# Weight conversion in a fused RWKV-6 and tanh-shrink kernel: the sign part is made by GpSimd instead of ScalarE

## The chip, the core and the metric

The kernel runs on one core of one Trainium2 chip. The metric is the device time of one launch in microseconds (us); lower is better. The engines are called by their profile names: PE is TensorE (PEld its weight loads), DVE is VectorE, ACT is ScalarE, POOL is GpSimd, and SP is SyncE, which here only starts DMAs.

## What is computed

Two blocks in sequence. The first is a linear-attention recurrence, the second a feed-forward block whose activation is `h - tanh(h)`.

```python
# r, k, v, w: (4, 8, 768, 48) float32;  u: (8, 48)
for t in range(S):
    cur = einsum('bhd,bhe->bhde', u[None] * kt, vt)
    y[:, :, t] = einsum('bhd,bhde->bhe', rt, state + cur)
    state = wt[:, :, :, None] * state + einsum('bhd,bhe->bhde', kt, vt)
x = y.transpose(0, 2, 1, 3).reshape(3072, 384)
h = x @ w_in                     # w_in (384, 2048)
out = (h - tanh(h)) @ w_out      # w_out (2048, 384)
```

The kernel is handed `w_in` and `w_out` as 64-bit words and makes float32 weights of them on the chip; that conversion is what the change is about.

## The kernel before

**Blocks and steps.** The 3,072 tokens are cut into eight blocks of 384. For each block, 16 feed-forward steps `f` run: `first` multiplies one slice of 128 columns of `w_in` with the block's `xT` (three matmuls of 384 columns, L871) and ScalarE copies the result out of PSUM as `h` (L876). VectorE squares it (`s`, L902), ScalarE makes `qa` of it (L905), VectorE makes `h` times a polynomial and then `g` from it (two instructions of L879), and TensorE multiplies `g` by a slice of `w_out` (L950 in the first block, a scheme with fewer products at L999 in the later ones). In the first block the second product of a step is queued three steps after its `g`. The attention work of the next block is laid between the steps: decay scans on VectorE (L417, L429), products (L436, L443, L382, L386), masked copies out of PSUM (L502), state updates (L587).

**Order.** PE, SP, DVE and ACT run in the order in which the program issues their instructions; it is written out by hand. Only POOL's queue is left to a scheduler; before the change it holds small fills, the drawing of masks, and three small DMAs (L777).

**The weights.** They arrive as 16 units of 768 columns (two slices of `w_in` or of `w_out`), one DMA each into a buffer `raw` (L251, five buffers), and stay in `w_sb` afterwards. All of this happens in the start-up (`boot`) and in the steps of the first block. A word of a unit has a low and a high half, each read with a stride of two 32-bit words. `convert` returns three ScalarE operations (L264) and one VectorE operation (L268) for a unit:

- `a`, into `w_sb`: the high half times `HIGH_SCALE`;
- `high`, a float16 in the one half of each word of a scratch tile `up` (four buffers): the high half times `SIGN_SCALE`, which leaves the sign;
- `low`, a uint16 in the other half of `up`: the low half scaled;
- on VectorE, `a` shifted left by three bits and joined with `up`, back into `w_sb`.

`converting(pieces, n)` issues the next `n` ScalarE operations of the units and says which VectorE operations have become due; those are issued in the next step, as `extra`. `PIECES` says how many operations each step of the first block issues. In `boot`, units 0 and 1 and most of unit 2 are converted.

Of the kernel before, what the change touches and what calls it, by code (L numbers as in the profile page):

```python
# [72 lines left out]
RAWS = 5  # L73
LAG = 2
LAST = 5
PIECES = 0, 0, 2, 3, 3, 3, 3, 4, 3, 3, 3, 4, 4
UNITS = [(0, 0), (0, 1)] + [u for j in range(NF // 2 - 2) for u in ((1, j), (0, j + 2))] + [(1, NF // 2 - 2),
                                                                                      (1, NF // 2 - 1)]
LATE = 3
# [47 lines left out]
def kernel(  # L127
# [12 lines left out]
    nc = tc.nc  # L140
# [112 lines left out]
    def convert(part, j, raw, _, tiles=1):  # L253

        lo, hi = raw[:, :, 0], raw[:, :, 1]
        a = w_sb[:, part, 2 * j:2 * j + 2].rearrange("p f c -> p (f c)").bitcast(I32)
        up = conv.tile([P, 2 * DM], I32, name="up", tag="up", bufs=4)
        low, high = (up.bitcast(t).rearrange("p (n two) -> p n two", two=2)[:, :, i]  # L260
                     for i, t in enumerate((U16, F16)))

        def scaled(to, of, scale, bias=0.0):
            return lambda: nc.scalar.activation(out=to, in_=of, func=AF.Copy, scale=scale, bias=bias)  # L264

        return [scaled(a.bitcast(F32), hi.bitcast(F32), HIGH_SCALE), scaled(high, hi.bitcast(F32), SIGN_SCALE),
                scaled(low, lo.bitcast(U32), *LOW)], [
                lambda of=slice(i * 2 * DM // tiles, (i + 1) * 2 * DM // tiles): nc.vector.scalar_tensor_tensor(  # L268
                    out=a[:, of], in0=a[:, of], scalar=3, in1=up[:, of], op0=ALU.logical_shift_left,
                    op1=ALU.bitwise_or) for i in range(tiles)]  # L270
# [49 lines left out]
    class Block:  # L320
# [411 lines left out]
        def together(self, ps):  # L732

            self.results(ps)
            yp, spread, St, ended = self.yp, isinstance(ps, Kept), states[self.q], {}

            def scores(p, c, h, par):
                toks = slice(64 * par, 64 * par + 64)
                return self.v[toks, c, p * D2 + h * D:p * D2 + (h + 1) * D], A[toks, h, p, c, :]

            def from_state(p, c, h, par):
                rows = slice(64 * h, 64 * h + D)
                return St[rows, p, 2 * c + par, 0:D], self.chunk("pre", p, 2 * c + par, spread)[rows]

            def stretch(of, cross):
                first = cross not in ended
                begun = set()
                for n in range(UP):
                    for c in range(NCP):
                        for h in range(2):  # L750
                            for x in range(2):
                                p, par = UP * n + x, x ^ cross
                                if of is from_state and not (self.q or c or par):
                                    continue
                                lhs, rhs = of(p, c, h, par)
                                e0, n0 = 64 * (h ^ x), (n * NCP + c) * L
                                done = nc.tensor.matmul(yp[x][e0:e0 + D, par, n0:n0 + L], lhsT=lhs, rhs=rhs,  # L757
                                                        start=first and (x, e0) not in begun, stop=True,
                                                        skip_group_check=True)
                                begun.add((x, e0))  # L760
                                if not first and len(begun) == 1:
                                    begin_behind(ended[cross], done)
                if first:
                    ended[cross] = nc.gpsimd.memset(ended_at, 0.0)
                    begin_behind(done, ended[cross])

            for of in (from_state, scores) if self.q else (scores, from_state):
                for cross in range(2):
                    stretch(of, cross)
            self.result_out(ALL)  # L770
            self.fill_holes([nc.sync])

        def fill_holes(self, engines, which=range(2 * KC)):
# [342 lines left out]
    def converting(pieces, n):  # L1116

        made = []
        for _ in range(n):
            if not pieces:  # L1120
                on_act, on_dve = convert(*raws.pop(0))
                pieces += zip(on_act, ([], [], on_dve))
            op, then = pieces.pop(0)
            op()
            made += then
        return made

    def boot(ps, pair, blk, later):
        h1, h2 = HALVES
        blk.tiles["w"] = states0  # L1130
        for name, p0, n in (("w", h1 + 1, 1), ("w", h1, 1), ("k", h1, UP), ("r", h1, UP), ("w", h2, UP)):
            blk.load(name, p0, n)
        blk.load_v()
        blk.load("k", h2, UP)
        blk.load("r", h2, UP)
        more_weights(nc.sync)

        both = (h1, h1 + 1), (h2, h2 + 1)
        blk.behind(h1 + 1, 1)
        blk.behind(h1, 1)  # L1140
        blk.take_whole(h1, UP)
        blk.totals_by_column(h1)
        nc.scalar.copy(out=later_ident, in_=ident)
        blk.before(h1, UP)
        blk.times_behind(h1, UP)
        blk.times_u(h1, UP)
        own = blk.own(ps, h1, spare=94, ahead=5, late=6)
        blk.turn_1(ps, h1)
        blk.times_before(h1, UP)
        earlier = blk.earlier(ps, h1)  # L1150
        blk.behind(h2, UP)
        blk.take_whole(h2, UP)
        first_a, first_b = convert(*raws.pop(0), tiles=2)
        own()
        blk.turn_2(h1)
        blk.totals_by_column(h2)
        blk.update_half(pair, h1)
        begin_behind(blk.done, more_weights(nc.sync))
        blk.times_behind(h2, UP)
        blk.times_u(h2, UP)  # L1160
        blk.turn_1(ps, h2)
        blk.turn_2(h2)
        earlier()
        blk.results(ps)
        blk.result("from_scores", both[0])
        run(blk.states_half(h1))
        blk.result("from_states", both[0], True, apart=True)
        blk.before(h2, UP)
        blk.update_half(pair, h2)
        blk.times_before(h2, UP)  # L1170
        own = blk.own(ps, h2)
        own_scored = blk.done
        run(first_a[:1])
        blk.result_out((3,), [nc.scalar.copy] * 2)
        blk.result_out((2,))
        earlier = blk.earlier(ps, h2, ahead=1)
        scored = blk.done
        onwards = blk.states_half(h2)
        own()
        run(first_a[1:])  # L1180
        needed = 2 * KC - 2
        blk.fill_holes([nc.sync, nc.gpsimd], range(needed, 2 * KC))
        begin_behind(own_scored, more_weights(nc.sync))
        blk.fill_holes([nc.sync, nc.gpsimd], range(needed))
        begin_behind(scored, more_weights(nc.sync))
        later.load("w")
        second_a, second_b = convert(*raws.pop(0))
        third_a, third_b = convert(*raws.pop(0))
        run(second_a)
        more_weights(nc.sync)  # L1190
        blk.results(ps)
        blk.yp.reverse()
        blk.result("from_states", both[1], apart=True)
        earlier(1, 1)
        earlier(0, 1)
        for p in reversed(both[1]):
            blk.result("from_scores", (p,), True, more=True)
        later.load("k")
        more_weights(nc.sync)
        run(onwards)  # L1200
        run(first_b[:1])
        for p in reversed(both[1]):
            blk.result_out((p,), [nc.scalar.copy, nc.vector.tensor_copy])
        run(first_b[1:])
        run(third_a[:2])
        run(second_b)
        blk.held(0, NPAIR)
        return [(third_a[2], third_b)]

    mains = ExitStack()  # L1210
    ps_a = Kept(mains.enter_context(tc.tile_pool(name="ps_a", bufs=1, space=PSUM)))
# [35 lines left out]
    for i, blk in enumerate(blocks):  # L1247
# [9 lines left out]
        for f in range(NF):  # L1257
# [21 lines left out]
            if not now:  # L1279
                ops = square + converting(pieces, 2)  # L1280
            elif now == 1:
                ops = rest + late + square + converting(pieces, 3)
            elif not i:
                ops = extra + square + (rest + behind + spare if f < 7 else rest[:1] + behind + spare + rest[1:])
            elif forming:
                ops = between(rest, forming[:2]) + square + formed + forming[2:]
                ops = (between(ops, behind) if len(behind) > 2 else ops + behind) + spare
            elif square:
                ops = (between(rest, behind) if len(behind) > 2 else rest + behind) + square + formed + extra + spare
            else:  # L1290
                ops = between(rest + formed, behind + spare)
# [161 lines left out]
```

## The times and the profile before

| what | value |
|---|---|
| median of 3 runs | 544.39 us (544.1 to 545.06) |
| the profiled execution, its own time | 545.07 us |
| its span in the trace | 543.3 us |
| granted TensorE clock | 1.0 throughout |
| PE busy | 534.1 us (98%) |
| DVE busy | 459.0 us (84%) |
| ACT busy | 403.7 us (74%) |
| POOL busy | 6.5 us (1%), 47 instructions |

The busy shares are means over stages that differ: the weights are converted in the first 80 us, and nothing of the change lies behind that. Matmuls are pipelined and their ends are modelled, so a busy PE says only that it had something in flight.

### The profile page before, as it was taken

Reading aid. Unit: us, or ns where it says so; the run is one execution under the profiler, and the core shown is the slowest. Engines: PE = TensorE matmul, PEld = TensorE weight load, DVE = VectorE, ACT = ScalarE, POOL = GpSimd, SP = SyncE. Lnnn points to the kernel's source line nnn. Section 1 sums busy time; section 2 is a strip of 40 time slices with the busy share of each in tenths; the row PEclk is TensorE's granted clock in tenths of the full one; section 3 lists DMA queues with packets and bytes.
Section 4 is the critical chain, followed back from the end, with each engine's and each line's share of the span. In section 5 each row is a group of like instructions: output and inputs, shape, how many; then the busy total and the mean of one; then the engine's idle time right before and its main releaser. Section 6 shows DMA issues by size and latency. Waiting matters only on the chain.

```text
span 543.3 us, 14866 instructions
## 1 busy us (share of the span) xinstructions
PE 534.1 (98%) x5682; PEld 403.3 (74%) x5682; DVE 459.0 (84%) x943; ACT 403.7 (74%) x814; POOL 6.5 (1%) x47
## 2 busy tenths in 40 slices
PE   7999999999999999999999999999999999999996
PEld 5756665678877777777887787877788788777874
DVE  7999999999989989798997979879797997557463
ACT  4899986888668876688767886688866885766561
POOL 1100000000000000000000000000000000000000
PEclk9999999999999999999999999999999999999999
DMA  7798732252311631154112532136321420100101
GB/s 276 234 402 311 259 119 74 97 137 63 122 42 54 162 118 57 43 147 119 60 56 87 122 103 70 48 97 151 84 89 46 122 27 3 56 1 0 45 1 46
DMA packets 53048, 56.34 MB, mean 104 GB/s; under 512 B 21488, under 2 KB 50928, under 8 KB 52976
## 3 DMA queue, kind: packets, MB, share of 16 engines
q1 hardware_dynamic: 52592, 55.18, 33.9%
q8 instruction: 48, 0.79, 0.6%
q14 instruction: 24, 0.20, 0.1%
q10 hardware_dynamic: 288, 0.10, 0.1%
q0 software_dynamic: 96, 0.07, 0.1%
HBM read 44.73 MB, written 4.72 MB: 91 GB/s over the span
## 4 chain that ended last, share of the span: by engine, by line
PE 88%; DVE 6%; ACT 2%; issue 2%; DMA 1%; SPq 0%; DVEq 0%
PE hp L871 41%; PE acc L999 27%; PE att L999 7%; PE att L757 4%; PE acc L950 3%; PE acc L977 2%; PE att L494 2%; PE att L575 1%; PE att L871 1%; ACT up L264 1%; DMA r<-in_rT 1%; DVE w_sb L268 1%; PE acc L871 1%; DVE scores L502 1%; DVE states L587 1%
## 5 line engine op out<-in xcount | busy, mean ns | idle before, releaser
L871 PE MATMUL hp<-xT,w_sb 128*128 128x384 f32 x738 | 259.3, 488 | 0.4 <-ACT h L876 0.4
L871 PEld LDWEIGHTS hp<-xT,w_sb 128*128 128x128 f32 x738 | 131.8, 190 | 70.0 <-ACT h L876 1.3
L999 PE MATMUL acc<-forms,g 128*128 128x128 f32 x954 | 133.2, 276 | 0.0
L876 ACT ACTIVATE h<-hp 128x384 f32<-128x384 f32 x123 | 60.3, 490 | 96.6 <-PE hp L871 96.5
L999 PEld LDWEIGHTS acc<-forms,g 128*128 128x128 f32 x954 | 122.0, 192 | 10.3
L879 DVE SCALAR_TENSOR_TENSOR h<-h,s 128x384 f32<-128x384 f32 x128 | 70.5, 551 | 51.9 <-ACT s L894 51.8
L920 DVE TENSOR_TENSOR g<-g 128x256 f32<-128x256 f32 x265 | 103.2, 418 | 7.4 <-PE acc L999 6.5
L895 ACT ACTIVATE qa<-s,shift 128x384 f32<-128x384 f32 x113 | 69.5, 615 | 3.7
L897 ACT ACTIVATE junk<-s,shift 128x384 bf16<-128x384 f32 x113 | 67.7, 599 | 0.0
L879 DVE SCALAR_TENSOR_TENSOR g<-qa,h 128x384 f32<-128x384 f32 x112 | 61.6, 550 | 1.6 <-ACT qa L905 0.2
L894 ACT ACTIVATE s<-h 128x384 f32<-128x384 f32 x113 | 59.2, 523 | 3.6
L999 PEld LDWEIGHTS acc<-w_sb,g 128*128 128x128 f32 x318 | 46.8, 191 | 9.7 <-ACT sums L967 0.3
L999 PE MATMUL acc<-w_sb,g 128*128 128x128 f32 x318 | 53.0, 276 | 0.0
L999 PE MATMUL att<-w_sb,g 128*128 128x128 f32 x212 | 35.5, 275 | 0.0
L999 PEld LDWEIGHTS att<-w_sb,g 128*128 128x128 f32 x212 | 31.1, 192 | 5.3
L1034 DVE TENSOR_TENSOR sums<-sums 128x256 f32<-128x256 f32 x84 | 32.8, 406 | 1.7 <-ACT sums L1011 1.4
L950 PE MATMUL acc<-w_sb,sums 128*128 128x384 f32 x96 | 33.9, 489 | 0.1
L264 ACT ACTIVATE up<-raw 128x768 f16<-128x768 f32 (+1 forms) x32 | 33.1, 1074 | 0.0
L950 PEld LDWEIGHTS acc<-w_sb,sums 128*128 128x128 f32 x96 | 17.9, 190 | 13.0 <-DVE sums L879 1.2
L417 DVE TENSOR_TENSOR_SCAN pre<-w,start 128x780 f32<-128x780 f32 x14 | 25.0, 1783 | 0.8
L429 DVE TENSOR_TENSOR_SCAN post<-w,seed 128x780 f32<-128x780 f32 x14 | 24.9, 1775 | 0.0
L897 ACT ACTIVATION_READ_ACCUMULATOR junk<-s,shift 128x1 f32 x113 | 21.1, 187 | 0.0
(118 smaller groups left out, 528.8 us busy)
## 6 DMA issues: line engine op xcount, KB each, us to landing
raw<-in_weights SPq DMA_DIRECT2D x16, 768.0 KB, 7.1
w<-in_wT SPq DMA_DIRECT2D x7, 780.0 KB, 4.7
k<-in_kT SPq DMA_DIRECT2D x7, 768.0 KB, 4.6
r<-in_rT SPq DMA_DIRECT2D x7, 768.0 KB, 4.6
v_sb<-in_v SPq DMA_DIRECT2D x8, 576.0 KB, 4.0
k<-in_tokens SPq DMA_DIRECT2D x7, 576.0 KB, 5.0
r<-in_tokens SPq DMA_DIRECT2D x7, 576.0 KB, 4.7
out_y<-sums SPq DMA_DIRECT2D x18, 128.0 KB, 1.8
```

Source lines behind the costliest of these rows:

```text
L264: return lambda: nc.scalar.activation(out=to, in_=of, func=AF.Copy, scale=scale, bias=bias)
L417: return nc.vector.tensor_tensor_scan(out=self.tile("pre")[:, cols], data0=self.tile("w")[:, cols], data1=start[:, 0:n * NCH * LP], initia ...
L871: nc.tensor.matmul(hp, lhsT=w_in_sb[:, f, kc, :], rhs=xT[kc], start=(kc == KC - 1), stop=(kc == 0))
L876: return h, nc.scalar.activation(out=h, in_=hp, func=AF.Copy, scale=1.0 / UPSCALE)
L879: return lambda: nc.vector.scalar_tensor_tensor(out=out, in0=in0, scalar=scalar, in1=in1, op0=op0, op1=ALU.mult)
L894: nc.scalar.activation(out=s, in_=h, func=AF.Square)
L895: nc.scalar.activation(out=qa, in_=s, func=AF.Square, bias=shift[:, 4:5])
L897: nc.scalar.activation(out=junk[:, 0:NB], in_=s, func=AF.Relu, bias=shift[:, 5:6], accum_out=excess[:, at:at + 1])
L920: return lambda: nc.vector.tensor_tensor(out=G[:, to:to + 2], in0=two(G, g_at(q, a0), g_at(q, a1)), in1=two(G, g_at(q, b0), g_at(q, b1)), ...
L950: nc.tensor.matmul(acc, lhsT=g[:, j * P:(j + 1) * P], rhs=w_out_sb[:, f, :], start=(f == self.first), stop=(f == NF - 1))
L999: nc.tensor.matmul(to, lhsT=G[:, g_at(q, a), :], rhs=rhs, start=start, stop=stop, skip_group_check=True)
L1034: ops.append(lambda op=op, at=at: nc.vector.tensor_tensor(out=at[0], in0=at[1], in1=at[2], op=OPS[op]))
```

## The change

The float16 multiplication that makes `high` is issued on POOL (`tensor_single_scalar`), together with ScalarE's operation for `a` as one entry of the list. A unit then has two entries instead of three. `PIECES` and the counts in `boot` and in the first two steps are scaled so that each unit's entries fall into the same steps as before; the VectorE operations of L268 keep their places in VectorE's order. An edit of `result_out` concerns only a call from the branch for unusual inputs, which isn't taken.

```diff
-PIECES = 0, 0, 2, 3, 3, 3, 3, 4, 3, 3, 3, 4, 4
+PIECES = 0, 0, 1, 2, 2, 2, 2, 2, 2, 2, 2, 3, 3
...
-        return [scaled(a.bitcast(F32), hi.bitcast(F32), HIGH_SCALE), scaled(high, hi.bitcast(F32), SIGN_SCALE),
-                scaled(low, lo.bitcast(U32), *LOW)], [
+        def signs():
+            nc.gpsimd.tensor_single_scalar(high, hi.bitcast(F32), SIGN_SCALE, op=ALU.mult)
+            scaled(a.bitcast(F32), hi.bitcast(F32), HIGH_SCALE)()
+
+        return [signs, scaled(low, lo.bitcast(U32), *LOW)], [
                 lambda of=slice(i * 2 * DM // tiles, (i + 1) * 2 * DM // tiles): nc.vector.scalar_tensor_tensor(
...
-            self.result_out(ALL)
+            self.result_out(ALL, None if spread else [nc.scalar.copy] * 2)
...
-                pieces += zip(on_act, ([], [], on_dve))
+                pieces += zip(on_act, ([], on_dve))
...
-        run(third_a[:2])
+        run(third_a[:1])
...
-        return [(third_a[2], third_b)]
+        return [(third_a[1], third_b)]
...
-                ops = rest + late + square + converting(pieces, 3)
+                ops = rest + late + square + converting(pieces, 2)
```

## The prediction

> **What bounds the kernel now.** I read the page first, for the span and the engines' busy time.
>
> ```profile
> span 543.3 us, 14866 instructions
> PE 534.1 (98%) x5682; PEld 403.3 (74%) x5682; DVE 459.0 (84%) x943; ACT 403.7 (74%) x814; POOL 6.5 (1%) x47
> ```
>
> TensorE is busy nearly always, but that is a mean. The conversions lie only in the first 80 us, so I asked next for the busy time of each engine in stretches, cut where the chain below changes its engine.
>
> ```profile
> core 0: us, PE busy (x) PEld busy (x) DVE busy (x) ACT busy (x) POOL busy (x), PEclk, DMA share, GB/s
> 31.70:76.10 44.40, 43.92 (x309) 26.20 (x307) 42.62 (x81) 43.52 (x63) 0.13 (x2) 1.00 0.76 277
> 23.50:39.70 16.20, 16.20 (x56) 9.00 (x50) 14.25 (x27) 14.65 (x21) 0.00 (x0) 1.00 1.01 381
> 39.70:50.50 10.80, 10.42 (x40) 6.45 (x41) 10.05 (x19) 10.80 (x17) 0.00 (x0) 1.00 1.00 378
> 50.50:76.10 25.60, 25.50 (x245) 15.25 (x244) 25.08 (x47) 25.60 (x38) 0.13 (x2) 1.00 0.58 193
> ...
> 100.00:500.00 400.00, 400.00 (x4312) 314.05 (x4311) 343.85 (x721) 299.15 (x634) 2.04 (x23) 1.00 0.30 79
> ```
>
> From 31.7 to 76.1 us three engines are full at once: PE lacks 0.48 us of 44.40, ACT 0.88, DVE 1.78. From 100 to 500 us PE lacks nothing, so a delay of PE that stands at 76 us is carried to the end, and so is a gain. Then the chain of work that ended last, in order of time, says which of the three full engines sets the pace.
>
> ```profile
> 37.73 1.95 PE att L871 x6
> 39.74 0.47 ACT h L876
> 40.21 0.81 ACT w_sb L264
> 41.02 0.97 ACT up L264
> ...
> 50.47 0.56 DVE sums L879
> ...
> 75.58 0.47 DVE sums L879
> 76.10 2.20 PE acc L950 x6
> ```
>
> The chain runs on PE up to 39.7 us, on ACT to 50.5 us (its conversions in `w_sb` and `up` are links of it), on DVE to 76.1 us, and on PE from there on. The reader is to see two things: ACT, which the change relieves, is the pacemaker for 11 us only, and DVE, which the change doesn't relieve, is the pacemaker for 26 us, with PE close behind both.
>
> **What is removed.** The costs are those of the groups of instructions with different shapes kept apart.
>
> ```profile
> L264 ACT ACTIVATE up<-raw 128x768 f16<-128x768 f32 x16 | 17.3, 1078 | 0.0
> L264 ACT ACTIVATE up<-raw 128x768 uint16<-128x768 uint32 x16 | 17.1, 1071 | 0.0
> L264 ACT ACTIVATE w_sb<-raw 128x768 f32<-128x768 f32 x16 | 14.8, 924 | 1.3 <-DMA raw<-in_weights 1.2
> ```
>
> The first row goes away: 16 instructions of 1.078 us, 17.3 us of ACT. On the path they can be worth no more than the time that PE isn't busy: 0.38 us between 39.7 and 50.5 us, 0.10 us between 50.5 and 76.1 us, 0 from 23.5 to 39.7 us. So 17.3 us off ACT are worth at most 0.5 us of the end. The other two rows, and VectorE's join, stay in their steps.
>
> **What is added.** Sixteen POOL instructions, 128x768, float32 in, float16 out. The trace of before has nothing like them; the nearest are POOL's own small ones.
>
> ```profile
> L171 POOL MEMSET start<- 128x780 f32 x1 | 0.8, 752 | 0.0
> L184 POOL TENSOR_SCALAR_AFFINE_SELECT mask_all<-mask_all 64x64 int8<-64x64 int8 x3 | 0.6, 232 | 0.0
> L200 POOL COPY mask_all<-mask_all 64x128 int8<-64x128 int8 x1 | 0.3, 284 | 0.1
> masks.py:199 POOL TENSOR_SCALAR_AFFINE_SELECT ident<-ident 128x128 f32<-128x128 f32 x1 | 0.3, 283 | 0.0
> masks.py:197 POOL MEMSET ident<- 128x128 f32 x1 | 0.2, 205 | 0.3 <-POOLq L1445 0.3
> ```
>
> The two fills give a line: (752 - 205) / (780 - 128) = 0.84 ns a column and 0.10 us at no columns. An instruction that only writes would so take 0.10 + 768 x 0.84 ns = 0.74 us, the lower end. The two that read and write 128 columns take 283 and 284 ns, (0.283 - 0.10) / 128 = 1.45 ns a column, so 768 columns take 1.21 us. The 64 columns of L184 give (0.232 - 0.10) / 64 = 2.1 ns a column, 1.7 us, the upper end. I take 1.21 us, since those two rows read, compute and write as the new one does. The Trainium skill (GPSIMD Engine Reference, Elementwise side-by-side cycle accounting) gives 1.03 cycles an element at 1.2 GHz for light bodies and 1.8 for a tight loop; an estimate from that page is 0.66 to 1.15 us, and the sums below would by it be 4.9 to 9.8 us where mine is 10.4.
>
> By its own length the new instruction is no bound: 16 of 1.21 us are 19 us on an engine with 0.13 us of work in the 44 us where most of them fall.
>
> **What it meets.** POOL's instruction waits only for its unit's DMA, for a free `up`, and for POOL's queue. Where DMAs are late, it starts with ACT's first conversion of the unit. These rows are ACT's timeline, the first and the last of twelve units:
>
> ```profile
> 31.73 0.94 ACT L264 ACTIVATE w_sb<-raw 128x768 f32<-128x768 f32 x1 [0.39 <-DMA raw<-in_weights]
> ...
> 74.08 0.93 ACT L264 ACTIVATE w_sb<-raw 128x768 f32<-128x768 f32 x1
> ```
>
> So units 4 to 15, twelve instructions, run beside a DVE that is busy 42.62 us of 44.40. The question on which the forecast hangs is whether DVE pays for that. The rows of before show what DVE's instructions read (groups in the window 31.7 to 76.1 us; L382 and L390 have as many columns, with two operands in SBUF and with one):
>
> ```profile
> L268 DVE SCALAR_TENSOR_TENSOR w_sb<-w_sb,up 128x768 int32<-128x768 int32 x11 | 10.4, 948 | 0.0
> L382 DVE TENSOR_TENSOR k<-k,u_row 128x1152 f32<-128x1152 f32 x1 | 1.3, 1349 | 0.0
> L390 DVE TENSOR_REDUCE diagonal<-k 128x24 f32<-128x1152 f32 x1 | 1.3, 1345 | 0.0
> L502 DVE COPY_PREDICATED scores<-mask_all,att 128x768 f32<-128x768 uint8 x2 | 1.9, 1013 | 0.0
> L587 DVE TENSOR_TENSOR states<-states,att 128x192 f32<-128x192 f32 x5 | 1.8, 353 | 0.3
> L902 DVE DVE_READ_ACCUMULATOR2_ANT top<- 128x1 f32 x11 | 0.9, 81 | 0.0
> L416 DVE RECIPROCAL start<-whole 128x12 f32<-128x12 f32 x2 | 0.4, 222 | 0.0
> L449 DVE TENSOR_SCALAR whole<-post 128x12 f32<-128x12 f32 x2 | 0.3, 174 | 0.1
> L465 DVE TENSOR_SCALAR holds<-whole 128x24 bf16<-128x24 f32 x1 | 0.2, 170 | 0.0
> ```
>
> A second operand costs DVE nothing (1349 ns against 1345), so it reads two streams of SBUF side by side. All rows here but L268 and L382 read at most one stream from SBUF: 1.3 + 1.9 + 1.8 + 0.9 + 0.4 + 0.3 + 0.2 = 6.8 us. The remaining 42.6 - 6.8 = 35.8 us, 84% of DVE's work, read two. No row shows POOL reading beside that. The bounds are 0 (POOL has a path of its own) and the full length of POOL's instruction (it reads on one of DVE's two paths, and a DVE instruction with two operands stands until it is through). I take the full end: the even price of two streams says that both paths are DVE's for such an instruction, and it leaves nothing over in 84% of its time. The Trainium skill (SBUF — State Buffer, Who interferes with whom) speaks against the change here: it says that GpSimd has no SBUF port beside VectorE's second pair, that a VectorE instruction with two SBUF inputs contends with a GpSimd instruction that reads SBUF, and that whoever starts first holds the pair for its whole length. No trace of before can show it.
>
> **The sum.** Twelve instructions x 1.21 us x 0.84 = 12.2 us more on DVE between 31.7 and 76.1 us. DVE's idle 1.78 us there takes some of it up (the gaps are waits for ACT's `qa`, which is early once DVE is late): 12.2 - 1.8 = 10.4 us. At 76.10 us PE waits for DVE's `g` with no slack, so it passes whole. Units 2 and 3 fall before 31.7 us, where DVE idles 1.95 us of 16.20 and PE paces: nothing. The start-up has a term of its own:
>
> ```profile
> 5.25 8.54 SPq L251 DMA_DIRECT2D raw<-in_weights  x2
> ...
> 9.42 1.77 DVE L429 TENSOR_TENSOR_SCAN post<-states,seed 128x780 f32<-128x780 f32 x1
> ...
> 12.36 0.96 DVE L443 TENSOR_TENSOR post<-k,post 128x768 f32<-128x768 f32 x1
> ...
> 17.39 1.57 POOL L777 DMA_DIRECT2D xT<-late  x3 [14.19 <-ACT late L729]
> ```
>
> Unit 0's DMA is issued at 5.25 us and its POOL instruction starts when that lands, somewhere in the chain of two-operand DVE work that leads to the first matmuls: 0 to 1.2 us, I take 0.6. It stands ahead of the three DMAs at 17.39 us on POOL's queue, and is long through by then. Unit 1's stands behind them, at about 19 us, where DVE works from PSUM: nothing. ACT's `low` now waits for POOL's instruction of the same unit, with `h` of the next step queued behind it and PE waiting for that `h`; between ACT's `a` and `low` lie `h` and `qa`, so 0.92 us of `a` and about 1 us more cover the 1.21 us. If POOL starts more than about 0.7 us late, that cover is gone and the rest is added to ACT, which has 1.08 us a unit to spare now.
>
> Total 10.4 + 0.6 = 11.0 us. Against the profiled execution, 545.07 + 11.0 = 556.1 us; that one lies 0.7 us over the median of the runs, 544.39, so the forecast of the median is 555.4 us. With POOL's instruction between 0.74 us (12 x 0.74 x 0.84 - 1.8 = 5.7) and 1.7 us (15.3, and 1.2 in the start-up), this case reaches from 550 to 561 us.
>
> **The rivals.**
>
> *No contention.* POOL reads beside DVE at no cost. ACT is relieved, and PE gets back at most its 0.48 us: 543.9 us, which can't be told from no change, as 0.2% or 1.1 us can't. For it: no row of before shows contention. Against: the two full streams. This is the rival on the other side, not slower; it decides if DVE's rows keep their lengths (L268 0.95 us) beside POOL's. More than 1.1 us faster would need PE time that isn't there.
>
> *Shared by the cycle.* DVE pays only for the cycles in which POOL reads, half of its length say: 12 x 0.6 x 0.84 - 1.8 + 0.3 = 4.5 us, 548.9 us (546 to 551). For it: POOL's rows take 1.45 ns a column where DVE's take 1.17 (1349 / 1152), so POOL wouldn't read all the time.
>
> *DVE keeps POOL out.* Its instructions follow without gaps, and POOL gets in only when DVE stops at the join (L268) for want of the signs. Then POOL's 1.21 us and ACT's `low`, 1.07 us, which waits for it, lie bare: 12 x 2.28 - 1.8 = 25.6 us, 570 us (564 with 0.74 us). Against: DVE has gaps and single-operand instructions every few us, in which POOL gets in.
>
> That the conversions don't move is no rival: in the changed program's order POOL has the 16, ACT lacks 16, and DVE's order is the same.
>
> **The numbers.** Full-length contention 0.58, shared 0.16, none 0.17, POOL kept out 0.09. All but the third are slower by over 0.2%; of the third 0.04 goes to faster, 0.13 to the same. The range from 546 to 570 us leaves out only the third case.
>
> **What would show it.** Right: DVE's two-operand rows longer, or gaps before them, by about 1 us a unit between 31 and 76 us; ACT with idle time there; the chain on DVE from about 32 us; PE short by some 10 us before 90 us and unchanged after. Wrong: DVE's rows as before; POOL's instruction above 1.7 us or below 0.74; ACT's `low` waiting on POOL.

## The result

| kernel | runs | median | lowest to highest |
|---|---|---|---|
| before | 4 | 544.54 us | 544.1 to 545.06 |
| changed | 4 | 552.11 us | 551.75 to 552.34 |

The ratio is 1.0128, with a 95% interval of 1.0101 to 1.0155: the changed kernel is 7.6 us slower. 555.4 us was forecast, 546 to 570 us as the range. The profiled execution of the changed kernel took 552.01 us, with a span of 550.3 us; 7.0 us more than the span before.

**The profile after.** Lines have moved by three: L271 is the join that was L268, L882 and L905 were L879 and L902, L452 was L449, L953 was L950. The new instruction is L267. First the span and its row among the costliest groups, then the busy time in the stretch that ends with the same matmul as the prediction's stretch from 31.7 to 76.1 us.

```profile
span 550.3 us, 14890 instructions
...
L267 POOL TENSOR_SCALAR up<-raw 128x768 f16<-128x768 f32 x16 | 43.0, 2710 | 29.1 <-DMA raw<-in_weights 18.3
```

```profile
core 0: us, PE busy (x) PEld busy (x) DVE busy (x) ACT busy (x) POOL busy (x), PEclk, DMA share, GB/s
31.70:83.00 51.30, 46.78 (x310) 26.87 (x309) 50.10 (x81) 35.27 (x52) 33.08 (x14) 0.97 0.66 239
...
110.00:500.00 390.00, 390.00 (x4261) 306.84 (x4260) 335.59 (x700) 291.89 (x617) 2.04 (x23) 1.00 0.30 81
```

DVE runs the same 81 instructions as before, busy for 50.10 us instead of 42.62: 7.48 us more. Its idle time falls from 1.78 to 1.20 us, 0.58 us less. 7.48 - 0.58 = 6.90 us, by which the stretch is longer. Behind it PE is full, as before, so the 6.9 us stay.

Which instructions became longer is seen in DVE's groups in this stretch (mean in ns in the middle column). Ahead of the dots are those that grew, behind them three of those that didn't.

```profile
L271 DVE SCALAR_TENSOR_TENSOR w_sb<-w_sb,up 128x768 int32<-128x768 int32 x11 | 11.1, 1009 | 0.0
L882 DVE SCALAR_TENSOR_TENSOR h<-h,s 128x384 f32<-128x384 f32 x10 | 8.3, 828 | 0.0
L905 DVE CUSTOM_DVE_ANT_0 s<-h 128x384 f32<-128x384 f32 x11 | 7.4, 671 | 0.0
L882 DVE SCALAR_TENSOR_TENSOR sums<-qa,h 128x384 f32<-128x384 f32 x10 | 6.5, 650 | 0.6
L420 DVE TENSOR_TENSOR_SCAN pre<-w,start 128x780 f32<-128x780 f32 x2 | 4.0, 2010 | 0.1
L452 DVE TENSOR_SCALAR whole<-post 128x12 f32<-128x12 f32 x2 | 1.4, 700 | 0.1
...
L590 DVE TENSOR_TENSOR states<-states,att 128x192 f32<-128x192 f32 x5 | 1.8, 353 | 0.3
L393 DVE TENSOR_REDUCE diagonal<-k 128x24 f32<-128x1152 f32 x1 | 1.3, 1346 | 0.0
L385 DVE TENSOR_TENSOR k<-k,u_row 128x1152 f32<-128x1152 f32 x1 | 1.3, 1345 | 0.0
```

A mean hides that the growth is not even. POOL's and DVE's timelines side by side show that for each POOL instruction one DVE instruction stands, that is, takes longer than its length. These are two of the twelve, POOL's row first:

```profile
69.97 2.69 POOL L267 TENSOR_SCALAR up<-raw 128x768 f16<-128x768 f32 x1 [4.61 <-DVE w_sb L271]
```

```profile
69.81 0.55 DVE L905 CUSTOM_DVE_ANT_0 s<-h 128x384 f32<-128x384 f32 x1
70.28 0.08 DVE L905 DVE_READ_ACCUMULATOR2_ANT top<- 128x1 f32 x1
70.28 1.25 DVE L882 SCALAR_TENSOR_TENSOR h<-h,s 128x384 f32<-128x384 f32 x1
71.45 1.34 DVE L385 TENSOR_TENSOR k<-k,u_row 128x1152 f32<-128x1152 f32 x1
```

```profile
31.44 2.68 POOL L267 TENSOR_SCALAR up<-raw 128x768 f16<-128x768 f32 x1 [1.73 <-DMA raw<-in_weights]
```

```profile
30.07 1.78 DVE L432 TENSOR_TENSOR_SCAN post<-w,seed 128x780 f32<-128x780 f32 x1
31.89 0.72 DVE L452 TENSOR_SCALAR whole<-post 128x12 f32<-128x12 f32 x1
```

L882 takes 1.25 us where 0.55 is its length, 0.70 us more; L385 behind it, still beside the same POOL instruction, has its full speed again. The instruction that already runs when POOL starts keeps its length too. So a POOL instruction of 2.7 us holds DVE up once, for 0.45 to 0.75 us. 7.48 us over twelve is 0.62 us each.

POOL seems to wait in its turn. At 24.16 us, beside two DVE copies out of PSUM, its instruction takes 2.41 us; the longest of the twelve takes 3.80 us, and it starts 0.20 us behind a two-operand scan of 1.77 us. L452 behind the scan then stands for 0.51 us:

```profile
35.68 3.80 POOL L267 TENSOR_SCALAR up<-raw 128x768 f16<-128x768 f32 x1 [1.56 <-DVE sums L882]
```

```profile
35.48 1.77 DVE L432 TENSOR_TENSOR_SCAN post<-w,seed 128x780 f32<-128x780 f32 x1
37.29 0.68 DVE L452 TENSOR_SCALAR whole<-post 128x12 f32<-128x12 f32 x1
```

By these rows whichever starts first is served first, and DVE stands for less than a third of POOL's length.

PE then waits for DVE's `g`, at three places of more than 0.9 us, the last of which ends the stretch:

```profile
41.00 2.20 PE L953 MATMUL acc<-w_sb,sums 128*128 128x384 f32 x6 [0.92 <-DVE sums L882]
...
61.80 3.13 PE L953 MATMUL acc<-w_sb,sums 128*128 128x384 f32 x6 [1.95 <-DVE sums L882]
...
83.00 2.20 PE L953 MATMUL acc<-w_sb,sums 128*128 128x384 f32 x6 [1.22 <-DVE sums L882]
```

No row of the waits has DVE or ACT waiting for POOL. Late weights are no cause either: ACT's conversions wait 1.4 us for the weights' DMAs, where they waited 1.2 us before. The chain that ended last does pass over POOL once, from 52.08 to 57.00 us, but only because the join at 57.00 us starts just as POOL's instruction ends; DVE has no gap before it.

### The profile page after: what moved, and what is told of

Read it like the earlier page. It is cut to its first block, busy times and chain, and to the rows that moved or that the text cites. A ratio compares the mean times of both kernels' runs of the same rounds, so it can differ in the third digit from the quotient of the medians.

```text
span 550.3 us, 14890 instructions
## 1 busy us (share of the span) xinstructions
PE 537.1 (98%) x5682; PEld 403.8 (73%) x5682; DVE 466.6 (85%) x943; ACT 391.2 (71%) x798; POOL 49.4 (9%) x63
## 4 chain that ended last, share of the span: by engine, by line
PE 85%; DVE 8%; issue 2%; DMA 2%; ACT 1%; POOL 1%; SPq 0%; DVEq 0%; ACTq 0%; POOLq 0%
PE hp L874 40%; PE acc L1002 26%; PE att L1002 6%; PE att L760 4%; PE acc L953 2%; PE acc L980 2%; PE att L497 2%; DVE w_sb L271 1%; PE att L578 1%; DVE h L882 1%; DMA raw<-in_weights 1%; DMA r<-in_rT 1%; DVE post L432 1%; DVE s L905 1%; POOL up L267 1%
## 5 line engine op out<-in xcount | busy, mean ns | idle before, releaser
L879 ACT ACTIVATE h<-hp 128x384 f32<-128x384 f32 x123 | 60.4, 491 | 105.7 <-PE hp L874 97.3
L882 DVE SCALAR_TENSOR_TENSOR h<-h,s 128x384 f32<-128x384 f32 x128 | 73.3, 573 | 51.5 <-ACT s L897 51.4
L882 DVE SCALAR_TENSOR_TENSOR g<-qa,h 128x384 f32<-128x384 f32 x112 | 61.6, 550 | 1.6 <-ACT qa L908 0.2
L267 POOL TENSOR_SCALAR up<-raw 128x768 f16<-128x768 f32 x16 | 43.0, 2710 | 29.1 <-DMA raw<-in_weights 18.3
L953 PE MATMUL acc<-w_sb,sums 128*128 128x384 f32 x96 | 35.1, 503 | 4.3 <-DVE sums L882 4.1
L953 PEld LDWEIGHTS acc<-w_sb,sums 128*128 128x128 f32 x96 | 17.9, 192 | 18.5 <-DVE sums L882 7.4
L420 DVE TENSOR_TENSOR_SCAN pre<-w,start 128x780 f32<-128x780 f32 x14 | 25.4, 1815 | 0.8
```

The lines of the kernel that those rows point to most:

```text
L267: nc.gpsimd.tensor_single_scalar(high, hi.bitcast(F32), SIGN_SCALE, op=ALU.mult)
L879: return h, nc.scalar.activation(out=h, in_=hp, func=AF.Copy, scale=1.0 / UPSCALE)
L882: return lambda: nc.vector.scalar_tensor_tensor(out=out, in0=in0, scalar=scalar, in1=in1, op0=op0, op1=ALU.mult)
L953: nc.tensor.matmul(acc, lhsT=g[:, j * P:(j + 1) * P], rhs=w_out_sb[:, f, :], start=(f == self.first), stop=(f == NF - 1))
```

## The experiments

Two theories were put against each other; a ratio below is that to the kernel before, with its 95% interval. **A (path):** DVE stands because POOL reads SBUF on a path that DVE's instruction needs. **B (lateness):** the signs are ready late, since POOL takes 2.7 us for them, and what waits for them runs late. The first four kernels shared 24 runs of the kernel before, median 544.69 us.

### POOL reads, and nobody waits

```diff
+        unused = conv.tile([P, 2 * DM], I32, name="unused", tag="unused", bufs=1)
+        aside = unused.bitcast(F16).rearrange("p (n two) -> p n two", two=2)[:, :, 1]
+        def beside():
+            nc.gpsimd.tensor_single_scalar(aside, hi.bitcast(F32), SIGN_SCALE, op=ALU.mult)
+            scaled(a.bitcast(F32), hi.bitcast(F32), HIGH_SCALE)()
-        return [scaled(a.bitcast(F32), hi.bitcast(F32), HIGH_SCALE), scaled(high, ...
+        return [beside, scaled(high, ...
```

> The kernel before with one thing added: POOL reads the high half of each unit as in the changed kernel, but writes into a scratch tile that nobody waits for; ScalarE still makes the signs. Theory A (path): VectorE stands about 0.6 us at each of the twelve POOL instructions that fall between 31 and 80 us because POOL reads SBUF, so 12 x 0.6 = 7.4 us, less some slack, are lost here too: 550.5 to 553 us, and twelve VectorE instructions are 0.45 to 0.75 us longer than their group. Theory B (lateness): the loss came from signs that are ready late (2.7 us on POOL) and from instructions waiting for them; here nobody waits, so 544.2 to 545.2 us and VectorE's rows are as before.

Measured: 552.41 us, ratio 1.0131 (1.0109 to 1.0153). That is the changed kernel's time, with ScalarE not relieved and no instruction waiting for POOL's result. B is out. It also follows that ScalarE's relief and the waits on POOL, which only the changed kernel has, together make no difference that shows. In the trace twelve DVE instructions stand again, 8.0 us in sum, and they are two-operand instructions and L456 (the former L449):

```profile
35.71 2.48 DVE L436 TENSOR_TENSOR_SCAN post<-w,seed 128x780 f32<-128x780 f32 x1
38.22 0.92 DVE L456 TENSOR_SCALAR whole<-post 128x12 f32<-128x12 f32 x1
...
53.44 1.25 DVE L886 SCALAR_TENSOR_TENSOR h<-h,s 128x384 f32<-128x384 f32 x1
...
59.71 2.45 DVE L443 TENSOR_TENSOR pre<-r,pre 128x1536 f32<-128x1536 f32 x1
```

### Half of the columns

```diff
-            nc.gpsimd.tensor_single_scalar(aside, hi.bitcast(F32), SIGN_SCALE, op=ALU.mult)
+            nc.gpsimd.tensor_single_scalar(aside[:, 0:DM], hi[:, 0:DM].bitcast(F32), SIGN_SCALE, op=ALU.mult)
```

> As the kernel with POOL reading beside, but POOL reads and writes 384 of the 768 columns. Theory A with a price by the column: the standing time of VectorE is about 0.3 us for each POOL instruction, so 12 x 0.3 = 3.7 us less the slack: 546.5 to 548.5 us. Theory A with a price by the instruction: as with 768 columns, 550.5 to 553 us. Theory B: 544.2 to 545.2 us.

Measured: 547.23 us, ratio 1.0053 (1.0029 to 1.0076): 2.5 us, within the range expected for a price by the column. POOL's timeline gives the length for 384 columns, DVE's the time that it stands:

```profile
47.02 1.36 POOL L270 TENSOR_SCALAR unused<-raw 128x384 f16<-128x384 f32 x1 [2.35 <-DMA raw<-in_weights]
...
70.40 1.59 POOL L270 TENSOR_SCALAR unused<-raw 128x384 f16<-128x384 f32 x1 [4.70 <-DMA raw<-in_weights]
```

```profile
59.69 0.88 DVE L886 SCALAR_TENSOR_TENSOR h<-h,s 128x384 f32<-128x384 f32 x1
...
70.73 1.69 DVE L393 TENSOR_TENSOR k<-k,r 128x1152 f32<-128x1152 f32 x1
```

0.88 - 0.55 = 0.33 us and 1.69 - 1.35 = 0.34 us, half of the 0.70 us with 768 columns. Not all twelve POOL instructions cost that: two scans lose about 0.1 us each, and beside the POOL instruction at 63.83 us nothing stands. In sum DVE's instructions grow by 3.05 us, against 8.0 with 768 columns. Some tenths of a microsecond of slack are taken off both, and so the loss falls to a third, not to a half.

### POOL writes and doesn't read

```diff
-            nc.gpsimd.tensor_single_scalar(high, hi.bitcast(F32), SIGN_SCALE, op=ALU.mult)
+            nc.gpsimd.memset(high, 0.0)
```

> The changed kernel, with a fill of zeros on POOL into the same columns in place of the multiplication; the signs of the weights are left out. POOL's queue, ScalarE's relief and every wait on POOL stay; POOL reads nothing. Theory A (reading): VectorE's rows are as before and only ScalarE's relief is left, worth at most 0.5 us by TensorE's free time: 543.9 to 544.7 us. Theory A' (any POOL instruction holds VectorE, a writing one too): at least 12 x 0.3 us: over 547 us. Theory B (lateness) expects 544 us too, since a fill of 768 columns is about 0.8 us.

Measured: 544.99 us, ratio 1.0003 (0.9985 to 1.0021), no difference that can be told. POOL still writes 768 columns for each unit, in 0.97 us. In the stretch every fill runs beside a two-operand L882, and DVE's rows there are those of before (L882 took 0.55 us):

```profile
L882 DVE SCALAR_TENSOR_TENSOR h<-h,s 128x384 f32<-128x384 f32 x11 | 6.1, 556 | 0.0
```

```profile
31.70:76.10 44.40, 44.15 (x312) 26.88 (x311) 43.20 (x81) 35.16 (x53) 8.79 (x11) 1.00 0.76 274
```

DVE's 43.20 us are more than the 42.62 of before because the matmul that ended the stretch at 76.10 us now starts at 75.64 us: the last 0.46 us are work that follows. The fill leaves out the multiplication together with the reading, and is shorter; a POOL instruction that reads without computing was not run.

One DVE instruction does stand beside the fills. It is L468 (L465 before), an operation with a scalar on 24 columns, ahead of the stretch, where two fills run from 25.60 to 27.44 us; before it took 0.17 us:

```profile
25.60 1.84 POOL L267 MEMSET up<- 128x768 f16 x2 [4.78 <-DVE w_sb L271]
```

```profile
26.26 1.21 DVE L468 TENSOR_SCALAR holds<-whole 128x24 bf16<-128x24 f32 x1
```

So the fills spare the two-operand instructions, but in this one instance an operation with a scalar stands for 1.04 us beside a POOL that only writes. The next instruction starts at 26.96 us, before L468 is through, and no cost shows.

This is also the change's best case, since ScalarE is relieved and nothing in the stretch stands. From 31.7 to 76.1 us ACT is busy for 35.16 us instead of 43.52, and the time stays the same. PE is busy for 44.15 of 44.40 us; there was next to nothing to win.

### Only the first four units

```diff
+            if UNITS.index((part, j)) < 4:
+                nc.gpsimd.tensor_single_scalar(high, hi.bitcast(F32), SIGN_SCALE, op=ALU.mult)
             scaled(a.bitcast(F32), hi.bitcast(F32), HIGH_SCALE)()
+            if UNITS.index((part, j)) >= 4:
+                scaled(high, hi.bitcast(F32), SIGN_SCALE)()
```

> The changed kernel, with POOL making the signs of units 0 to 3 only; ScalarE makes those of units 4 to 15 as before. Theory A: those four POOL instructions lie before 31 us, where VectorE works from PSUM, idles or isn't what TensorE waits for, so nothing of the loss is left: 544.2 to 545.2 us. If a part of the loss comes from the start-up (my prediction had 0.6 us there) it shows here as that much.

Measured: 545.28 us, ratio 1.0009 (0.9996 to 1.0022): not told from the kernel before, and its profiled span is 543.0 us. The loss belongs to units 4 to 15. A few tenths of a microsecond in the start-up can be neither shown nor excluded.

### The disputed instructions by themselves

A kernel of its own, each of its three forms run once: VectorE runs stages of 24 equal instructions, POOL forty signs beside them; then the same without POOL's, and then with POOL's instruction reading and writing adjacent float32.

```python
nc.vector.tensor_tensor(out=two_in, in0=x, in1=y, op=ALU.mult)                    # 24 times, two SBUF operands
nc.vector.tensor_reduce(out=small, in_=x.rearrange(...), op=ALU.add, ...)         # 24 times, one
nc.vector.tensor_tensor(out=from_psum, in0=acc, in1=x[:, 0:512], op=ALU.mult)     # 24 times, PSUM and SBUF
nc.vector.tensor_single_scalar(scaled, x, 0.5, op=ALU.mult)                       # 24 times, one SBUF operand
nc.gpsimd.tensor_single_scalar(up[:, :, 1], raw[:, :, 1].bitcast(F32), 2.0 ** -64, op=ALU.mult)   # 40 times
```

> Not the computation, only the disputed instructions; the output is a fill. VectorE runs 8 products of two SBUF operands (128x768) alone, then 24 of them, then 24 reductions with one SBUF operand, 24 products of a PSUM and a SBUF operand (128x512) and 24 multiplications of one SBUF operand by a scalar (128x768), back to back, while POOL makes 40 signs back to back. Theory A (path, two operands): the 24 two-operand products lengthen from about 0.95 us, in sum by about 0.6 us for each POOL instruction that runs beside them; reductions and products from PSUM keep their lengths. The multiplication by a scalar is open: one 12-column instruction of this kind stood 0.5 us in the changed kernel, so I expect it to be held as well. POOL's instruction is 2.4 us beside one-operand work and 2.7 us or more beside two-operand work. Theory B (lateness alone) expects the same VectorE lengths in all stages as alone.

> The measurement of the instructions alone, without POOL's signs: the lengths of VectorE's five stages with nothing beside them. Theory A: the 32 two-operand products are about 0.95 us each where beside POOL they were 1.21 in the mean; reductions 0.95 and products from PSUM 0.69 as beside POOL; the multiplications by a scalar, 0.97 us beside POOL, are clearly shorter alone if they are held as well, and 0.97 us if not. Theory B: all lengths as beside POOL.

> The measurement beside POOL again, with POOL reading 768 adjacent float32 and writing 768 adjacent float32, instead of every second word in and every second half-word out. If the price to VectorE is that of the columns read, the two-operand products still stand 0.54 us for each POOL instruction. If it is that of the words passed over, about half. POOL's own length is open: if strides and the conversion made it 2.4 us, it falls towards 1.2 us, the value that I took from the small instructions in the profile of before.

The eight products that were to run alone ahead of the stages ran beside POOL too (9.44 us, against 7.84 without POOL), so the lengths alone are those of the second form. VectorE's timeline, the four stages (start, length of the stage): alone, beside POOL's signs, beside POOL's adjacent words.

```profile
11.30 23.77 DVE L41 TENSOR_TENSOR two_in<-x,y 128x768 f32<-128x768 f32 x24
34.99 23.66 DVE L50 TENSOR_REDUCE small<-x 128x24 f32<-128x768 f32 x24
58.56 17.35 DVE L53 TENSOR_TENSOR from_psum<-acc,x 128x512 f32<-128x512 f32 x24
75.83 14.23 DVE L55 TENSOR_SCALAR scaled<-x 128x768 f32<-128x768 f32 x24
```

```profile
12.89 30.21 DVE L41 TENSOR_TENSOR two_in<-x,y 128x768 f32<-128x768 f32 x24
43.02 23.66 DVE L50 TENSOR_REDUCE small<-x 128x24 f32<-128x768 f32 x24
66.59 17.35 DVE L53 TENSOR_TENSOR from_psum<-acc,x 128x512 f32<-128x512 f32 x24
83.86 24.16 DVE L55 TENSOR_SCALAR scaled<-x 128x768 f32<-128x768 f32 x24
```

```profile
12.79 29.81 DVE L41 TENSOR_TENSOR two_in<-x,y 128x768 f32<-128x768 f32 x24
...
83.36 19.65 DVE L55 TENSOR_SCALAR scaled<-x 128x768 f32<-128x768 f32 x24
```

Reductions and products from PSUM aren't touched, to the hundredth of a microsecond. The two-operand products lose 30.21 - 23.77 = 6.44 us to the twelve POOL instructions of that stage, 0.54 us each; taken singly, every second one takes 1.49 us, the others 0.96. The multiplications by a scalar, which read one operand, lose 9.93 us to eight, 1.24 us each: the kind of L452 is held too, and worse. Taken singly, two of them stand for each POOL instruction, one near its start (0.53 us more than the 0.56 alone) and one that runs past its end (0.71 us more), here with POOL's row first:

```profile
90.88 2.94 POOL L38 TENSOR_SCALAR up<-raw 128x768 f16<-128x768 f32 x1
```

```profile
91.24 1.09 DVE L55 TENSOR_SCALAR scaled<-x 128x768 f32<-128x768 f32 x1
92.36 0.56 DVE L55 TENSOR_SCALAR scaled<-x 128x768 f32<-128x768 f32 x1
92.96 1.27 DVE L55 TENSOR_SCALAR scaled<-x 128x768 f32<-128x768 f32 x1
```

A two-operand product stands only once, near POOL's start. That POOL reads near its start and writes near its end would fit both, and the fills, which only write, spared the products and held L468; the order within POOL's instruction is inferred. POOL's own groups in these stages:

```profile
L38 POOL TENSOR_SCALAR up<-raw 128x768 f16<-128x768 f32 x12 | 29.2, 2437 | 1.0
...
L38 POOL TENSOR_SCALAR up<-raw 128x768 f16<-128x768 f32 x10 | 23.9, 2386 | 0.8
...
L38 POOL TENSOR_SCALAR up<-raw 128x768 f16<-128x768 f32 x8 | 23.5, 2937 | 0.7
```

Beside two-operand work POOL takes 2.44 us, beside reductions 2.39, beside multiplications by a scalar 2.94. I had expected 2.7 us or more in the first of these, and that was wrong: VectorE pays there, POOL hardly. With adjacent words the two-operand products lose 6.04 us to twelve, 0.50 us each, so for them the price is that of the columns read and not of the words passed over. The multiplications by a scalar lose 0.49 us at each place, less than beside the signs, and eleven stand until POOL's forty end at 98.44 us, 5.42 us in sum. POOL's length then is 2.13 us beside reductions: strides and the conversion to float16 make 0.26 us of the 2.39, and it doesn't come near 1.2 us.

## Why the prediction was right, and where it wasn't

**What bounds the kernel: right.** The chain leaves PE for DVE, DVE's delay reaches PE whole, and PE can't make it up behind 83 us. The worth of ScalarE's relief, at most 0.5 us, was right too: in the run with the fill it doesn't show in the time.

**That DVE pays: right**, and so are the instructions that pay, but for two. L449 reads one operand and was put among the free ones; it is of the kind that is held (174 ns became 700). Here that is two instructions in twelve. That ACT's `low` waits for POOL's instruction of the same unit was wrong: unit 5's `low` starts at 36.85 us, while POOL's instruction runs from 35.68 to 39.48 us.

**POOL's length: wrong by a factor of two.** 1.21 us were worked out from two instructions of 128 columns, at 1.45 ns a column. Measured are 2.39 us beside work that doesn't disturb it, and from 1.36 us for 384 columns and 2.44 us for 768 beside two-operand work, about 2.8 ns a column. The upper end, 1.7 us from the row of 64 columns, didn't hold it either, and a length above it was one of the prediction's own signs of being wrong. The Trainium skill's figures (GPSIMD Engine Reference, Elementwise side-by-side cycle accounting), from which I estimated 0.66 to 1.15 us, are further off, and the measurement decides.

**How long DVE stands: wrong by a factor of nearly four, the other way.** The likeliest case let DVE stand for all of POOL's instruction, 84% of the time. With the measured 2.7 us it would have given 12 x 2.7 x 0.84 - 1.8 = 25.4 us. DVE stands for 0.62 us of the 2.7, 23%, and that makes 7.5 us. So the case that I took as the likeliest is refuted. Of the rivals "shared" comes nearest: DVE pays for a part of POOL's length, and that part follows the columns that POOL reads (0.33 us for 384, 0.70 for 768, nothing for a fill). Its half of 1.21 us, 0.6 us, was the right price for the wrong reason, and it isn't shared cycle by cycle: DVE stands in one block and then runs at full speed beside the rest of POOL's instruction. The step that failed is the choice between the bounds: even prices of one and two streams say which instructions need both paths, but not for how long POOL takes one of them. That POOL reads in this block and computes or writes after it is inferred; no trace shows what it does within an instruction. Nor is it shown why some instructions stand for 0.5 us and others for 0.7.

The Trainium skill (SBUF — State Buffer, Who interferes with whom) names instructions that contend and that these runs show standing: those with two SBUF inputs, and multiplications by a scalar, which can run in a mode that uses both ports (that they did so here no run shows). It excepts reductions, which kept 23.66 us, and an instruction with one SBUF input beside its PSUM operand, which kept 17.35, and for two SBUF inputs a GpSimd instruction that only writes, as with the fill. It says that who comes first holds the pair for its whole instruction; here VectorE stood for 0.45 to 0.75 us of 2.4 to 3.8, and the measurement decides.

**The slack: 1.8 us put, 0.6 us found.** I took all of DVE's gaps for waits on `qa`. The group of `g` of the kernel before, in the stretch from 31.7 to 76.1 us, shows that it was 1.0 us at most:

```profile
L879 DVE SCALAR_TENSOR_TENSOR sums<-qa,h 128x384 f32<-128x384 f32 x10 | 5.5, 554 | 1.2 <-ACT qa L905 1.0
```

In the changed kernel the same group has 0.6 us of idle time before it, and none of it waits for ACT. That halving is the 0.6 us of the stretch's 1.78; the other gaps stayed.

**The start-up: 0.6 us put, nothing found.** Unit 0's POOL instruction runs from 15.35 to 17.80 us. DVE first works from PSUM there, and its next instruction with two SBUF operands starts 0.82 us behind POOL's and keeps the 1.78 us of before:

```profile
16.17 1.78 DVE L420 TENSOR_TENSOR_SCAN pre<-states,start 128x780 f32<-128x780 f32 x1
```

The instruction was not through before the three DMAs on POOL's queue, as I had thought: these start at 17.69 us instead of 17.39. The first matmuls move from 23.50 to 23.55 us.

Sum by the measured terms: 7.5 - 0.6 = 6.9 us, the difference of the spans being 7.0. That 11.0 us came as near to the 7.6 us of the result is luck in part: two errors, a length too small and a share too large, work against each other.

## What to carry to other kernels

Before work is moved to an idle engine, ask what the busy engine beside it shares with it: an idle engine isn't a free path. Price such a move by instructions that meet, not by busy time, and take the price of one instruction from a measurement of the pair, since here neither the length from small instructions nor the share from reasoning was right. And first work out what the relieved engine could give back: 17 us less ScalarE work were worth at most the 0.5 us in which TensorE was free.

## What hadn't been expected

Of the four kinds measured by themselves, the multiplication by a scalar with one SBUF operand suffers most beside POOL: two stand for each POOL instruction, 1.24 us together, against 0.54 us for a product of two operands; alone it is also the fastest, 14.23 us for 24 where the product takes 23.77.

In the profiled execution, TensorE's granted clock is 0.83 between 60 and 70 us, where PE has just waited 1.95 us: the matmul group at 61.80 us takes 3.13 us instead of 2.20. It seems to have cost nothing, as PE waits for DVE again at 83.00 us, and runs with a mean clock of 0.994 and of 0.998 took the same time (552.01 and 552.21 us, 551.75 and 552.34 us). Why the clock fell wasn't examined.
